# Decode signs, low parts and gate denominators on GpSimd in a windowed attention and rational FFN kernel

## The chip, the cores and the metric

The kernel runs on one core of one Trainium2 chip. The metric is the device time of one execution in microseconds; lower is better. Engines are named as in the profile: PE is TensorE (matrix products), DVE is VectorE, ACT is ScalarE, POOL is GpSimd, SP is SyncE, which issues all transfers here. Tiles lie in SBUF; matrix products land in PSUM.

## The reference, cut to what matters

Eight batches of eight heads attend over 576 positions of 64 dimensions, causally and within a window of 64. The attention output, 4608 tokens by 512, goes through a feed-forward layer of 2048 with a rational function as its gate.

```python
# attention
mask = (rel >= 0) & (rel < window)               # window = 64
scores = np.where(mask, scale * q @ k.T, -1e9)
attn = softmax(scores)
x = (attn @ v)                                   # 4608 x 512 after the heads are joined
# feed-forward
h = x @ w_in                                     # 512 x 2048
P = a[0] + a[1]*h + a[2]*h**2 + a[3]*h**3
Q = 1.0 + np.abs(b[0])*np.abs(h) + np.abs(b[1])*h**2
g = P / (Q + 1e-6)
return (g @ w_out).astype(np.float32)            # 2048 x 512
```

`w_in` and `w_out` are float64; everything else is float32.

## The kernel before, in words

Tokens are worked through in 12 chunks of 384 (`CH`), `c` = 0 to 11. A chunk has four attention units (`hp`, two heads each) and 16 feed-forward steps (`i`, 128 of the 2048 inner columns each). A unit computes scores into PSUM, adds the mask and takes row maxima (L185 to L206; in chunks 1 and 2, `PEM`, the mask is added by TensorE), exponentials with row sums on ScalarE (L210, L213), reciprocals and the scaling of the tile `sm` (L215 to L217), transposes on TensorE, and the product with v. Its result x is kept as two float32r parts, `xh` and `xl`.

A step (`ffn1`) multiplies x with a column block of `w_in` in three passes of high and low parts, 12 matrix products into the PSUM tile `h`. Then comes the gate: ScalarE makes |h|, a3 h + a2 and the start of the denominator, `u` (L258 to L260); VectorE makes the numerator from `h` in PSUM (L261, L262); `u` is multiplied by |h| (L264), on VectorE for the first 28 gates (`DEC`) and on GpSimd for the rest; ScalarE turns it into a reciprocal by logarithm and exponential (L267, L268); VectorE makes the gate's high and low parts `gh` and `gl` (L269 to L272). Three steps later (`LAG`) `ffn2` multiplies them with a row block of `w_out`, nine matrix products into three PSUM tiles `o` (L292). At a chunk's end ScalarE copies `o` out, or VectorE adds it to a part sum (L299 to L306). The phases run chunk 0's first half, chunk 1's first half, chunk 1's second half, chunk 0's second half, then chunks 2 to 11 whole.

Weights are float64 and are turned into two float32r parts on the chip, in 32 tiles (16 of each matrix), by `decode`: a transfer into `w_st` (two buffers), on ScalarE the magnitude of the high word scaled by a power of two (L117), on VectorE a left shift (L119), the low word's top bits (L120) and the sign bit (L121) into `w_c`, on ScalarE the high part (L124), on VectorE the rest (L125). Eight such tiles of each matrix are asked for in the first steps, the rest one per step from step 7 on; a list `todo` tells at which step each load and each attention unit is written. The order on each engine is then set by a scheduler that runs when the kernel is built; on the chip each engine works through its own queue in order.

Of the kernel before, what the change touches and what calls it, by code (L numbers as in the profile page):

```python
# [9 lines left out]
F32 = mybir.dt.float32  # L10
F32R = mybir.dt.float32r
U32 = mybir.dt.uint32
AF = mybir.ActivationFunctionType
ALU = mybir.AluOpType
# [3 lines left out]
CH = 384  # L18
TC = CH // WIN
PR = TC // 2  # L20
DEC = 28
AHEAD = 3
LAG = 3
W_AT = 0, 1, 2, 3
# [7 lines left out]
def swa_rational_ffn(ctx: ExitStack, tc: tile.TileContext, qT, kT, v, w_in, w_out, a, b, out):  # L32
    nc = tc.nc
    P = 128
# [9 lines left out]
    SCALE = 1.0 / math.sqrt(64)  # L44
# [50 lines left out]
    nc.scalar.copy(out=ident_r, in_=ident)  # L95


    wi_h = const.tile([P, NCC, DFF], F32R, name="wi_h")
    wi_l = const.tile([P, NCC, DFF], F32R, name="wi_l")
    wo_h = const.tile([P, NF, DO], F32R, name="wo_h")  # L100
    wo_l = const.tile([P, NF, DO], F32R, name="wo_l")
    w_out_v = w_out.rearrange("(fc p) e -> p fc e", p=P)

    def decode(src, hi, lo):

        w = stage.tile([P, 512, 2], U32, name="w_st", bufs=2)
        if len(src.shape) == 3:
            nc.sync.dma_start(out=w.rearrange("p (c n) two -> p c (n two)", c=src.shape[1]), in_=src)
        else:
            nc.sync.dma_start(out=w.rearrange("p n two -> p (n two)"), in_=src)  # L110
        low, high = w[:, :, 0], w[:, :, 1]
        c = stage.tile([P, 512], U32, name="w_c")
        cf = c.bitcast(F32)

        nc.scalar.activation(cf, w.bitcast(F32)[:, :, 1], AF.Abs, scale=2.0 ** -111)  # L117

        nc.vector.tensor_scalar(out=c, in0=c, scalar1=3, scalar2=None, op0=ALU.logical_shift_left)  # L119
        nc.vector.scalar_tensor_tensor(out=c, in0=low, scalar=29, in1=c, op0=ALU.logical_shift_right, op1=ALU.bitwise_or)  # L120
        nc.vector.scalar_tensor_tensor(out=c, in0=high, scalar=0x80000000, in1=c, op0=ALU.bitwise_and, op1=ALU.bitwise_or)  # L121
        if len(hi.shape) == 3:
            cf = cf.rearrange("p (c n) -> p c n", c=hi.shape[1])
        nc.scalar.activation(hi, cf, AF.Copy, scale=2.0 ** -8)  # L124
        nc.vector.scalar_tensor_tensor(out=lo, in0=cf, scalar=2.0 ** -8, in1=hi.bitcast(F32), op0=ALU.mult, op1=ALU.subtract)  # L125

# [2 lines left out]
        decode(w_in[i], wi_h[:, :, sl], wi_l[:, :, sl])  # L129

    def load_w_out(i):
        decode(w_out_v[:, i, :], wo_h[:, i, :], wo_l[:, i, :])

    xh, xl = {}, {}
    live = {}
# [37 lines left out]
    def unit_scores(c, hp):  # L173
        u = live[c, hp]

        ps = ps_a.tile([P, 2, 512], F32, name="ps_s", bufs=1)
        m0 = u["m0"]
        on_pe = c in PEM
        if m0 is None:
            mm = mask[:, 1:2, :].broadcast_to([P, PR, P])  # L180
        else:
            mm = mask[:, m0:m0 + PR, :]
        if on_pe:
            for z in range(2):
                nc.tensor.matmul(ps[:, z, 0:PR * P].rearrange("p (r c) -> p r c", c=P), ident_r, mm, start=True, stop=False)  # L185
        for p in range(PR):
            for z in range(2):
                for e in range(2):
                    j = 2 * p + e
                    k = u["kt"][z * 64:z * 64 + 64].rearrange("p t s -> p (t s)")  # L190
                    w = u["kw"][j] * WIN
                    nc.tensor.matmul(ps[e * 64:e * 64 + 64, z, p * P:(p + 1) * P], u["q"][z * 64:z * 64 + 64, j, :],  # L192
                                     k[:, w:w + P], start=not on_pe, stop=not on_pe or p == PR - 1)
        sm = att.tile([P, 2 * PR, P], F32, name="sm")
        NR = 2 * PR
        nmx = att.tile([P, NR], F32, name="nmx")
        if on_pe:
            pss = ps[:, :, 0:PR * P].rearrange("p z (r c) -> p z r c", c=P)
            nc.vector.tensor_reduce(out=nmx.rearrange("p (z r) -> p z r", z=2), in_=pss, axis=AX.X, op=ALU.max, negate=True)
            nc.vector.tensor_scalar(out=nmx, in0=nmx, scalar1=SCALE, scalar2=None, op0=ALU.mult)  # L200
        else:
            for z in range(2):
                nc.vector.scalar_tensor_tensor(out=sm[:, z * PR:(z + 1) * PR, :],
                                               in0=ps[:, z, 0:PR * P].rearrange("p (r c) -> p r c", c=P), scalar=SCALE,
                                               in1=mm.bitcast(F32), op0=ALU.mult, op1=ALU.add)
            nc.vector.tensor_reduce(out=nmx, in_=sm, axis=AX.X, op=ALU.max, negate=True)  # L206
        sums = att.tile([P, NR], F32, name="sums")
        for j in range(NR):
            if on_pe:
                nc.scalar.activation(sm[:, j, :], ps[:, j // PR, (j % PR) * P:(j % PR + 1) * P], AF.Exp, scale=SCALE,  # L210
                                     bias=nmx[:, j:j + 1], accum_out=sums[:, j:j + 1])
            else:
                nc.scalar.activation(sm[:, j, :], sm[:, j, :], AF.Exp, bias=nmx[:, j:j + 1], accum_out=sums[:, j:j + 1])  # L213
        rs = att.tile([P, NR], F32, name="rs")
        nc.vector.tensor_scalar(out=sums, in0=sums, scalar1=1e-9, scalar2=None, op0=ALU.add)  # L215
        nc.vector.reciprocal(out=rs, in_=sums)  # L216
        (nc.vector if c < 2 else nc.gpsimd).tensor_tensor(out=sm, in0=sm, in1=rs.unsqueeze(2).broadcast_to([P, NR, P]), op=ALU.mult)  # L217
        u["sm"] = sm

    def unit_transpose(c, hp):  # L220
# [20 lines left out]
        nc.vector.tensor_tensor(out=xl[c, hp], in0=x, in1=xh[c, hp].bitcast(F32), op=ALU.subtract)  # L241

    gs = {}
    n_gates = [0]

    def ffn1(c, i):
        h = ps_h.tile([P, CH], F32, name="h")
        n = 0
        for cc in range(NCC):
            for w, x in ((wi_h, xl), (wi_h, xh), (wi_l, xh)):  # L250
                nc.tensor.matmul(h, w[:, cc, i * P:(i + 1) * P], x[c, cc], start=n == 0, stop=n == 3 * NCC - 1)  # L251
                n += 1
        ah = tmp.tile([P, CH], F32, name="ah")
        u = tmp.tile([P, CH], F32, name="u")
        num = tmp.tile([P, CH], F32, name="num")
        gh = gp.tile([P, CH], F32R, name="gh")
        gl = gp.tile([P, CH], F32R, name="gl")
        nc.scalar.activation(ah, h, AF.Abs)  # L258
        nc.scalar.activation(num, h, AF.Identity, scale=a_sb[:, 3:4], bias=a_sb[:, 2:3])  # L259
        nc.scalar.activation(u, ah, AF.Identity, scale=b_sb[:, 1:2], bias=b_sb[:, 0:1])  # L260
        nc.vector.tensor_tensor(out=num, in0=num, in1=h, op=ALU.mult)  # L261
        nc.vector.scalar_tensor_tensor(out=num, in0=num, scalar=a_sb[:, 1:2], in1=h, op0=ALU.add, op1=ALU.mult)  # L262
        n_gates[0] += 1
        (nc.vector if n_gates[0] <= DEC else nc.gpsimd).tensor_tensor(out=u, in0=u, in1=ah, op=ALU.mult)  # L264


        nc.scalar.activation(ah, u, AF.Ln, bias=QADD)  # L267
        nc.scalar.activation(ah, ah, AF.Exp, scale=-1.0)  # L268
        nc.vector.scalar_tensor_tensor(out=gh, in0=num, scalar=a_sb[:, 0:1], in1=ah, op0=ALU.add, op1=ALU.mult)  # L269
        nc.vector.scalar_tensor_tensor(out=u, in0=u, scalar=QADD, in1=gh.bitcast(F32), op0=ALU.add, op1=ALU.mult)  # L270
        nc.vector.scalar_tensor_tensor(out=num, in0=num, scalar=a_sb[:, 0:1], in1=u, op0=ALU.add, op1=ALU.subtract)  # L271
        nc.vector.tensor_tensor(out=gl, in0=num, in1=ah, op=ALU.mult)  # L272
        gs[c, i] = gh, gl
# [8 lines left out]
    def ffn2(s):  # L282
        c, i = steps[s]
        first = s == 0 or steps[s - 1][0] != c
        last = s == total - 1 or steps[s + 1][0] != c
        if first:
            acc[c] = [ps_o.tile([P, DO], F32, name=f"o{t}") for t in range(NTS)]
        gh, gl = gs.pop((c, i))
        for t in range(NTS):
            ts = slice(t * P, (t + 1) * P)  # L290
            for n, (g, w) in enumerate(((gl, wo_h), (gh, wo_l), (gh, wo_h))):
                nc.tensor.matmul(acc[c][t], g[:, ts], w[:, i, :], start=first and n == 0, stop=last and n == 2)  # L292
        if not last:
            return
        o = acc.pop(c)
        if c == 0 and c not in part:
            part[c] = const.tile([P, NTS, DO], F32, name="part")
            for t in range(NTS):
                nc.scalar.copy(out=part[c][:, t, :], in_=o[t])  # L299
            return  # L300
        for t in range(NTS):
            ob = part[0][:, t, :] if s == total - 1 else op.tile([P, DO], F32, name="ob")
            if c in part:
                nc.vector.tensor_tensor(out=ob, in0=o[t], in1=part[c][:, t, :], op=ALU.add)
            else:
                nc.scalar.copy(out=ob, in_=o[t])  # L306
            nc.sync.dma_start(out=out[c * CH + t * P:c * CH + (t + 1) * P, :], in_=ob)

    NU = HP
# [93 lines left out]
```

## Time and profile before

| | us |
|---|---|
| median of 3 runs | 1017.18 (1016.14 to 1017.22) |
| profiled execution | 1016.97 |
| its span, first to last instruction | 1015.2 |
| TensorE busy | 950.6 |
| VectorE busy | 837.1 |
| ScalarE busy | 723.9 |
| GpSimd busy | 233.2 |
| mean granted TensorE clock | 0.984 |

In the profile's rows a group stands as line, engine, operation, tile written <- tiles read, shape, count, then busy us and mean ns of one, then the engine's idle time just before such instructions with what ended it. In the 40 slices each digit is a busy share in tenths. A row of the waits has the waiting engine and line, what it waited for, the total in us, the number of times and the longest. In a timeline row the first two numbers are start and duration in us.

### The profile page before, as it was taken

The numbers are of one execution on the slowest core, as the hardware profiler recorded it, in microseconds if no ns is written. First come the engines' busy times: TensorE is split into PE (matmuls) and PEld (weight loads), VectorE is DVE, ScalarE is ACT, GpSimd is POOL, SyncE is SP. The second block draws the span as 40 slices with busy tenths as digits, with TensorE's granted clock in tenths as the row PEclk, the third lists the DMA queues.
The fourth block names the chain that finished last, engine by engine and source line by source line (L and its number), as shares of the span: only waits on it lengthen the run. The fifth ranks groups of instructions, "written<-read, shape, count | busy, mean of one in ns | idle before, by whom it ended". The sixth has DMA issues, their size and how long they took to land.

```text
span 1015.2 us, 18235 instructions
## 1 busy us (share of the span) xinstructions
PE 950.6 (94%) x6640; PEld 839.4 (83%) x6640; DVE 837.1 (82%) x1599; ACT 723.9 (71%) x1736; POOL 233.2 (23%) x231
## 2 busy tenths in 40 slices
PE   2668768999999999999999999999999999999997
PEld 2556557988888988988988888988988888888996
DVE  5999899887988887788888888788788888877875
ACT  4677676666677777777777777777777777776664
POOL 2000000003223223223223223223223222222221
PEclk9979889999999999999999999999999999999998
DMA  6653540020121121120121111120121121100000
GB/s 192 201 168 130 171 151 17 1 76 31 60 61 30 61 64 33 65 60 30 61 61 31 62 63 34 64 61 29 60 60 32 62 62 34 65 17 1 32 1 31
DMA packets 37816, 64.08 MB, mean 63 GB/s; under 512 B 4448, under 2 KB 24928, under 8 KB 37728
## 3 DMA queue, kind: packets, MB, share of 16 engines
q1 hardware_dynamic: 37728, 62.93, 19.7%
q8 instruction: 52, 0.85, 0.4%
q14 instruction: 36, 0.29, 0.1%
HBM read 53.48 MB, written 9.44 MB: 62 GB/s over the span
## 4 chain that ended last, share of the span: by engine, by line
PE 78%; DVE 11%; ACT 5%; DMA 4%; issue 2%; POOL 0%; SPq 0%; POOLq 0%; ACTq 0%; DVEq 0%
PE o L292 35%; PE h L251 34%; PE ps_x L235 3%; PE ps_s L192 3%; PE ps_s L224 2%; DMA w_st<-w_in 2%; DVE gh L269 1%; DMA w_st<-w_out 1%; ACT sm L213 1%; DVE u L270 1%; DVE w_c L120 1%; DVE num L271 1%; DVE w_c L121 1%; ACT w_c L117 1%; DVE gl L272 1%
## 5 line engine op out<-in xcount | busy, mean ns | idle before, releaser
L251 PE MATMUL h<-xl,wi_h 128*128 128x384 f32 x768 | 265.7, 346 | 18.7 <-DVE num L262 15.3
L251 PE MATMUL h<-xh,wi_l 128*128 128x384 f32 x768 | 260.5, 339 | 0.0
L251 PE MATMUL h<-xh,wi_h 128*128 128x384 f32 x768 | 260.1, 339 | 0.0
L292 PE MATMUL o<-wo_h,gl 128*128 128x512 f32 x576 | 232.3, 403 | 15.0 <-DVE gl L272 15.0
L264 POOL TENSOR_TENSOR u<-u,ah 128x384 f32<-128x384 f32 x164 | 168.4, 1027 | 326.3 <-ACT u L260 286.2
L292 PE MATMUL o<-wo_h,gh 128*128 128x512 f32 x576 | 229.2, 398 | 0.0
L292 PE MATMUL o<-wo_l,gh 128*128 128x512 f32 x576 | 228.1, 396 | 0.0
L261 DVE TENSOR_TENSOR num<-num,h 128x384 f32<-128x384 f32 x192 | 106.1, 553 | 105.9 <-ACT num L259 105.1
L258 ACT ACTIVATE ah<-h 128x384 f32<-128x384 f32 x192 | 94.3, 491 | 115.0 <-PE h L251 86.8
L251 PEld LDWEIGHTS h<-xl,wi_h 128*128 128x128 f32 x768 | 145.8, 190 | 28.0 <-DVE num L262 18.1
L217 POOL TENSOR_TENSOR sm<-sm,rs 128x768 f32<-128x768 f32 x40 | 59.4, 1484 | 443.8 <-DVE rs L216 421.6
L251 PEld LDWEIGHTS h<-xh,wi_h 128*128 128x128 f32 x768 | 145.9, 190 | 4.2
L251 PEld LDWEIGHTS h<-xh,wi_l 128*128 128x128 f32 x768 | 145.6, 190 | 0.6 <-issue 0.2
L292 PEld LDWEIGHTS o<-wo_h,gl 128*128 128x128 f32 x576 | 109.3, 190 | 42.1 <-DVE gl L272 17.2
L213 ACT ACTIVATE sm<-sm,nmx 128x128 f32<-128x128 f32 x240 | 93.3, 390 | 62.7 <-DVE nmx L206 62.7
L269 DVE SCALAR_TENSOR_TENSOR gh<-num,a_sb,ah 128x384 fp32r<-128x384 f32 x192 | 117.2, 621 | 24.8 <-ACT ah L268 24.6
L260 ACT ACTIVATE u<-ah,b_sb 128x384 f32<-128x384 f32 x192 | 136.1, 710 | 0.0
L292 PEld LDWEIGHTS o<-wo_h,gh 128*128 128x128 f32 x576 | 109.5, 190 | 23.6
L259 ACT ACTIVATE num<-h,a_sb 128x384 f32<-128x384 f32 x192 | 128.3, 668 | 0.0
L292 PEld LDWEIGHTS o<-wo_l,gh 128*128 128x128 f32 x576 | 109.7, 190 | 18.9
L262 DVE SCALAR_TENSOR_TENSOR num<-num,a_sb,h 128x384 f32<-128x384 f32 x192 | 117.6, 613 | 5.4
L271 DVE SCALAR_TENSOR_TENSOR num<-num,a_sb,u 128x384 f32<-128x384 f32 x192 | 116.1, 618 | 0.5
(51 smaller groups left out, 1109.1 us busy)
## 6 DMA issues: line engine op xcount, KB each, us to landing
out<-ob SPq DMA_DIRECT2D x33, 256.0 KB, 2.4
w_st<-w_in SPq DMA_DIRECT2D x16, 512.0 KB, 4.2
w_st<-w_out SPq DMA_DIRECT2D x16, 512.0 KB, 3.7
q<-qT SPq DMA_DIRECT2D x32, 192.0 KB, 3.3
vt<-v SPq DMA_DIRECT2D x16, 384.0 KB, 3.1
vt<-v SPq DMA_DIRECT2D x16, 320.0 KB, 3.1
kt<-kT SPq DMA_DIRECT2D x16, 224.0 KB, 3.5
kt<-kT SPq DMA_DIRECT2D x16, 192.0 KB, 3.7
```

Of the source, the lines that this page charges most:

```text
L213: nc.scalar.activation(sm[:, j, :], sm[:, j, :], AF.Exp, bias=nmx[:, j:j + 1], accum_out=sums[:, j:j + 1])
L217: (nc.vector if c < 2 else nc.gpsimd).tensor_tensor(out=sm, in0=sm, in1=rs.unsqueeze(2).broadcast_to([P, NR, P]), op=ALU.mult)
L251: nc.tensor.matmul(h, w[:, cc, i * P:(i + 1) * P], x[c, cc], start=n == 0, stop=n == 3 * NCC - 1)
L258: nc.scalar.activation(ah, h, AF.Abs)
L259: nc.scalar.activation(num, h, AF.Identity, scale=a_sb[:, 3:4], bias=a_sb[:, 2:3])
L260: nc.scalar.activation(u, ah, AF.Identity, scale=b_sb[:, 1:2], bias=b_sb[:, 0:1])
L261: nc.vector.tensor_tensor(out=num, in0=num, in1=h, op=ALU.mult)
L262: nc.vector.scalar_tensor_tensor(out=num, in0=num, scalar=a_sb[:, 1:2], in1=h, op0=ALU.add, op1=ALU.mult)
L264: (nc.vector if n_gates[0] <= DEC else nc.gpsimd).tensor_tensor(out=u, in0=u, in1=ah, op=ALU.mult)
L269: nc.vector.scalar_tensor_tensor(out=gh, in0=num, scalar=a_sb[:, 0:1], in1=ah, op0=ALU.add, op1=ALU.mult)
L271: nc.vector.scalar_tensor_tensor(out=num, in0=num, scalar=a_sb[:, 0:1], in1=u, op0=ALU.add, op1=ALU.subtract)
L292: nc.tensor.matmul(acc[c][t], g[:, ts], w[:, i, :], start=first and n == 0, stop=last and n == 2)
```

## The change

Four things move. In `decode`, ScalarE copies the high word with its sign instead of taking its magnitude; GpSimd multiplies the high words by zero in place, which leaves the sign bit alone; the left shift and the setting of the sign become one VectorE instruction, so that two VectorE passes remain of three. For `w_out`, ScalarE's high part is a plain copy and GpSimd subtracts it to get the low part; both stay 256 times too large, and the factor is taken out where PSUM is emptied. The multiplication of L264 is done by GpSimd for all gates. The scaling of `sm` in chunk 1 goes to GpSimd as that of the later chunks does. Two small VectorE instructions with a constant take a tile of zeros as second operand.

```diff
+    zero = const.tile([P, 2 * PR], F32, name="zero")
+    nc.vector.memset(zero, 0.0)
...
-    def decode(src, hi, lo):
+    def decode(src, hi, lo, scaled=False):
...
-        nc.scalar.activation(cf, w.bitcast(F32)[:, :, 1], AF.Abs, scale=2.0 ** -111)
-
-        nc.vector.tensor_scalar(out=c, in0=c, scalar1=3, scalar2=None, op0=ALU.logical_shift_left)
+        highf = w.bitcast(F32)[:, :, 1]
+        nc.scalar.activation(cf, highf, AF.Copy, scale=2.0 ** -111)
+
+        nc.gpsimd.tensor_scalar(out=highf, in0=highf, scalar1=0.0, scalar2=None, op0=ALU.mult)
+        nc.vector.scalar_tensor_tensor(out=c, in0=c, scalar=3, in1=high, op0=ALU.logical_shift_left, op1=ALU.bitwise_or)
         nc.vector.scalar_tensor_tensor(out=c, in0=low, scalar=29, in1=c, op0=ALU.logical_shift_right, op1=ALU.bitwise_or)
-        nc.vector.scalar_tensor_tensor(out=c, in0=high, scalar=0x80000000, in1=c, op0=ALU.bitwise_and, op1=ALU.bitwise_or)
...
+        if scaled:
+            nc.scalar.copy(out=hi, in_=cf)
+            nc.gpsimd.tensor_tensor(out=lo, in0=cf, in1=hi.bitcast(F32), op=ALU.subtract)
+            return
...
-        decode(w_out_v[:, i, :], wo_h[:, i, :], wo_l[:, i, :])
+        decode(w_out_v[:, i, :], wo_h[:, i, :], wo_l[:, i, :], scaled=True)
...
-            nc.vector.tensor_scalar(out=nmx, in0=nmx, scalar1=SCALE, scalar2=None, op0=ALU.mult)
+            nc.vector.scalar_tensor_tensor(out=nmx, in0=nmx, scalar=SCALE, in1=zero, op0=ALU.mult, op1=ALU.add)
...
-        nc.vector.tensor_scalar(out=sums, in0=sums, scalar1=1e-9, scalar2=None, op0=ALU.add)
+        nc.vector.scalar_tensor_tensor(out=sums, in0=sums, scalar=1e-9, in1=zero, op0=ALU.add, op1=ALU.add)
...
-        (nc.vector if c < 2 else nc.gpsimd).tensor_tensor(out=sm, ...)
+        (nc.vector if c < 1 else nc.gpsimd).tensor_tensor(out=sm, ...)
...
-        n_gates[0] += 1
-        (nc.vector if n_gates[0] <= DEC else nc.gpsimd).tensor_tensor(out=u, in0=u, in1=ah, op=ALU.mult)
+        nc.gpsimd.tensor_tensor(out=u, in0=u, in1=ah, op=ALU.mult)
...
-                nc.scalar.copy(out=part[c][:, t, :], in_=o[t])
+                nc.scalar.activation(part[c][:, t, :], o[t], AF.Copy, scale=2.0 ** -8)
...
-                nc.vector.tensor_tensor(out=ob, in0=o[t], in1=part[c][:, t, :], op=ALU.add)
+                nc.vector.scalar_tensor_tensor(out=ob, in0=o[t], scalar=2.0 ** -8, in1=part[c][:, t, :], op0=ALU.mult, op1=ALU.add)
             else:
-                nc.scalar.copy(out=ob, in_=o[t])
+                nc.scalar.activation(ob, o[t], AF.Copy, scale=2.0 ** -8)
```

More of the change, by code (lines that the diff above doesn't have):

```diff
@@ L20 @@
 PR = TC // 2
-DEC = 28
 AHEAD = 3
@@ L214, in unit_scores @@
         rs = att.tile([P, NR], F32, name="rs")
-        nc.vector.tensor_scalar(out=sums, in0=sums, scalar1=1e-9, scalar2=None, op0=ALU.add)
+        nc.vector.scalar_tensor_tensor(out=sums, in0=sums, scalar=1e-9, in1=zero, op0=ALU.add, op1=ALU.add)
         nc.vector.reciprocal(out=rs, in_=sums)
-        (nc.vector if c < 2 else nc.gpsimd).tensor_tensor(out=sm, in0=sm, in1=rs.unsqueeze(2).broadcast_to([P, NR, P]), op=ALU.mult)
+        (nc.vector if c < 1 else nc.gpsimd).tensor_tensor(out=sm, in0=sm, in1=rs.unsqueeze(2).broadcast_to([P, NR, P]), op=ALU.mult)
         u["sm"] = sm
@@ L243, in swa_rational_ffn @@
     gs = {}
-    n_gates = [0]
     def ffn1(c, i):
```

## The prediction

> **What bounds the kernel now.** I read the page's totals and its 40 slices first, to see where TensorE isn't full, then busy times by stretch, then who waited for whom there, then the groups on VectorE, then single instructions of GpSimd beside those of VectorE.
>
> ```profile
> PE 950.6 (94%) x6640; PEld 839.4 (83%) x6640; DVE 837.1 (82%) x1599; ACT 723.9 (71%) x1736; POOL 233.2 (23%) x231
> PE   2668768999999999999999999999999999999997
> DVE  5999899887988887788888888788788888877875
> POOL 2000000003223223223223223223223222222221
> ```
>
> TensorE (PE) is full from the seventh slice on. Only the first six (25.4 us each) have holes, and there VectorE (DVE) is at 9 while GpSimd (POOL) has nothing after the mask. The same by stretch:
>
> ```profile
> core 0: us, PE busy (x) PEld busy (x) DVE busy (x) ACT busy (x) POOL busy (x), PEclk, DMA share, GB/s
> 10.00:52.00 42.00, 23.68 (x237) 18.75 (x238) 38.38 (x72) 26.90 (x80) 0.00 (x0) 1.00 0.62 189
> 52.00:163.00 111.00, 79.84 (x545) 66.20 (x545) 105.27 (x207) 78.59 (x195) 3.31 (x2) 0.88 0.43 139
> 163.00:240.00 77.00, 77.00 (x465) 68.10 (x464) 66.84 (x126) 51.10 (x115) 5.38 (x4) 1.00 0.10 31
> 240.00:950.00 710.00, 709.25 (x5088) 633.12 (x5087) 579.25 (x1112) 528.23 (x1276) 204.40 (x185) 1.00 0.16 49
> ```
>
> From 163 us on TensorE has no holes, so nothing that the change does there can shorten the run. All its effect comes from 10 to 163 us, where VectorE is busy 38.4 of 42 and 105.3 of 111 us. That VectorE is what TensorE waits for in the second of these, and ScalarE (ACT) too:
>
> ```profile
> PE h L251 <- DVE num L262: 15.3, 6, 6.3
> PE o L292 <- DVE gl L272: 12.0, 4, 4.6
> ACT wo_h L124 <- DVE w_c L121: 8.6, 6, 2.7
> ```
>
> TensorE's idle time there is 111 - 79.8 = 31.2 us, and 27.3 of it are these two VectorE releasers. So in this stretch a microsecond of VectorE is about a microsecond of the run, until ScalarE (78.6 us) or TensorE (79.8 us) is the next bound.
>
> The VectorE groups of 52 to 163 us that the change touches, or that matter below:
>
> ```profile
> L121 DVE SCALAR_TENSOR_TENSOR w_c<-w_st,w_c 128x512 uint32<-128x512 uint32 x21 | 14.2, 683 | 0.0
> L120 DVE SCALAR_TENSOR_TENSOR w_c<-w_st,w_c 128x512 uint32<-128x512 uint32 x21 | 14.1, 684 | 0.0
> L119 DVE TENSOR_SCALAR w_c<-w_c 128x512 uint32<-128x512 uint32 x21 | 8.8, 421 | 4.0 <-ACT w_c L117 4.0
> L125 DVE SCALAR_TENSOR_TENSOR wo_l<-w_c,wo_h 128x512 fp32r<-128x512 f32 x13 | 8.8, 678 | 0.1
> L262 DVE SCALAR_TENSOR_TENSOR num<-num,a_sb,h 128x384 f32<-128x384 f32 x14 | 8.3, 606 | 0.0
> L261 DVE TENSOR_TENSOR num<-num,h 128x384 f32<-128x384 f32 x14 | 7.5, 547 | 0.6 <-ACT num L259 0.5
> L264 DVE TENSOR_TENSOR u<-u,ah 128x384 f32<-128x384 f32 x13 | 7.1, 549 | 0.0
> L199 DVE TENSOR_REDUCE nmx<-ps_s 128x6 f32<-128x768 f32 x6 | 5.7, 950 | 0.0
> L217 DVE TENSOR_TENSOR sm<-sm,rs 128x768 f32<-128x768 f32 x4 | 3.8, 952 | 0.0
> L241 DVE TENSOR_TENSOR xl<-ps_x,xh 128x384 fp32r<-128x384 f32 x4 | 2.2, 550 | 0.0
> ```
>
> By itself this says that the change helps. What speaks against it is seen only in single instructions. Here are the two GpSimd instructions of that stretch, one of the later part, and the VectorE instructions beside them (start, duration):
>
> ```profile
> 132.92 0.65 DVE L125 SCALAR_TENSOR_TENSOR wo_l<-w_c,wo_h 128x512 fp32r<-128x512 f32 x1
> 133.19 1.72 POOL L217 TENSOR_TENSOR sm<-sm,rs 128x768 f32<-128x768 f32 x1 [124.82 <-DVE rs L216]
> 133.49 1.96 DVE L125 SCALAR_TENSOR_TENSOR wi_l<-w_c,wi_h 128x512 fp32r<-128x512 f32 x1
> ...
> 154.90 1.60 POOL L217 TENSOR_TENSOR sm<-sm,rs 128x768 f32<-128x768 f32 x1 [20.00 <-DVE rs L216]
> 155.08 1.83 DVE L270 SCALAR_TENSOR_TENSOR u<-u,gh 128x384 f32<-128x384 f32 x1
> ...
> 236.60 0.62 DVE L262 SCALAR_TENSOR_TENSOR num<-num,a_sb,h 128x384 f32<-128x384 f32 x1
> 237.06 1.02 POOL L264 TENSOR_TENSOR u<-u,ah 128x384 f32<-128x384 f32 x1 [2.65 <-ACT u L260]
> 237.43 1.06 DVE L269 SCALAR_TENSOR_TENSOR gh<-num,a_sb,ah 128x384 fp32r<-128x384 f32 x1 [0.21 <-ACT ah L268]
> ...
> 238.61 0.56 DVE L270 SCALAR_TENSOR_TENSOR u<-u,gh 128x384 f32<-128x384 f32 x1
> 239.74 0.61 DVE L269 SCALAR_TENSOR_TENSOR gh<-num,a_sb,ah 128x384 fp32r<-128x384 f32 x1
> ```
>
> GpSimd's multiply at 133.19 ends at 134.91. The VectorE subtraction begun at 133.49 takes 1.96 us instead of about 0.68 and ends at 135.45: it stood still until GpSimd was done. The second case is the same (1.83 instead of 0.56, ending 0.41 us after GpSimd's 156.50), and so is L269 at 237.43 (1.06 instead of 0.61, ending 0.41 us after 238.08). L262 at 236.60, which reads h from PSUM, is not lengthened by the GpSimd multiply that begins in it. So in these rows a VectorE instruction with both inputs in SBUF and a GpSimd instruction don't run together, and VectorE pays up to the whole GpSimd duration. The Trainium skill, "SBUF — State Buffer", section "Who interferes with whom", states it as a rule: a VectorE instruction with two SBUF inputs contends with a GpSimd instruction that reads SBUF, the later one standing until the first is done; the trace agrees, with 1.96 for 0.68 us. By the same page the faster modes of VectorE's one-input instructions contend too, which would make the removal of the 421 ns shift a gain of its own; no run here shows that.
>
> **The change, part by part.** What moves goes to an engine that is slower at it and that stops VectorE while it runs. Start-to-start, a VectorE instruction costs some 0.08 us less than its duration (133.49 against 132.92 + 0.65), which I take off each. Counts are those of 52 to 163 us.
>
> - Signs: three VectorE passes per tile become two. L119 goes, and the new first pass is a 684 ns one like L120. Relief 21 x (0.42 - 0.08) = 7.2 us.
> - w_out's low parts: 13 x (0.68 - 0.08) = 7.8 us.
> - Denominators (L264): 13 x (0.55 - 0.08) = 6.1 us.
> - The softmax scaling of chunk 1 (L217, the change has c < 1 for c < 2): 4 x (0.95 - 0.08) = 3.5 us.
>
> Relief 24.6 us, leaving VectorE 105.3 - 24.6 = 80.7 us. Added to GpSimd, by its own rows:
>
> ```profile
> L264 POOL TENSOR_TENSOR u<-u,ah 128x384 f32<-128x384 f32 x164 | 168.4, 1027 | 326.3 <-ACT u L260 286.2 <-PE ps_s L192 33.5 <-DVE num L261 5.8
> L217 POOL TENSOR_TENSOR sm<-sm,rs 128x768 f32<-128x768 f32 x40 | 59.4, 1484 | 443.8 <-DVE rs L216 421.6 <-ACT ah L258 22.2
> L78 POOL TENSOR_SCALAR_AFFINE_SELECT sm<-sm 64x128 f32<-64x128 f32 x10 | 2.9, 288 | 0.3
> L69 POOL MEMSET sm<- 128x640 f32 x1 | 0.6, 631 | 0.3 <-POOLq L393 0.3
> masks.py:197 POOL MEMSET ident<- 128x128 f32 x1 | 0.2, 204 | 0.1
> ```
>
> - 13 denominators x 1.02 = 13.3 us; 4 scalings x 1.47 = 5.9 us.
> - 13 low parts of 512 columns: at least a denominator's 1.03 us, at most 512/384 of it, 1.37. I take 1.27, as two full inputs are nearest to L264: 16.5 us.
> - 21 signs, one input, 512 columns at every other word. From below 0.5 us (the fill's 631 x 512/640), from above 1.37 (the two-input pace). The select has one input as well: 0.29 us at 128 columns, and the two fills give 0.83 ns for each further column, so 0.61 at 512. I take 0.65: 13.7 us. The Trainium skill, "GPSIMD Engine Reference", section 7, gives some 1.9 cycles per element for reads of this step; estimated from it the sign is 0.81 us, which would add 2.2 us to the result below; no run here shows it.
>
> Together 49.4 us of GpSimd. Call f the part of it for which VectorE stands. Relief and blocking cancel at f = 24.6 / 49.4 = 0.50. The rows give f from 0.44 (L269: 1.06 - 0.61 of 1.02, where the rest fell on L262) to 0.87 (1.96 - 0.68 of 1.47). VectorE can work unharmed only in what reads at most one operand from SBUF: L261, L262, L199 and L241, without the 0.08, make 6.5 + 7.4 + 5.2 + 1.9 = 21.0 us, to which its 5.7 idle us come; so even the best packing leaves f = (49.4 - 26.7) / 49.4 = 0.46. I take 0.65, the middle of 0.44 and 0.87, since the instructions around a decode are mostly of the blocked kind. The stretch becomes 80.7 + 0.65 x 49.4 + 5.7 = 118.5 us, 7.5 longer. At f = 0.46 it is 1.9 us shorter, at 0.87 18.4 longer.
>
> The stretch to 52 us, by the same durations:
>
> ```profile
> L119 DVE TENSOR_SCALAR w_c<-w_c 128x512 uint32<-128x512 uint32 x11 | 4.7, 424 | 12.2 <-ACT w_c L117 12.2
> L125 DVE SCALAR_TENSOR_TENSOR wo_l<-w_c,wo_h 128x512 fp32r<-128x512 f32 x4 | 2.7, 684 | 0.0
> ```
>
> Relief 11 x 0.34 + 4 x 0.60 = 6.2 us; GpSimd 11 x 0.65 + 4 x 1.27 = 12.2 us; at 0.65 this is 7.9 - 6.2 = 1.7 longer (-0.6 to +4.4).
>
> Edits at nothing: the denominators after 163 us lie under a full TensorE; without that cover each of the remaining 15 would cost what it does above. The small six-column instructions change form, not number. ScalarE's Abs becomes a Copy of the same size; the 2^-8 at PSUM's emptying rides on instructions that are there already, and so on full TensorE, three of the last chunk excepted. No transfer is added, but the sign is one more step ahead of the release of w_st, which the load two tiles on waits for, with the q, k and v loads queued behind that load on SyncE, and of all that is queued behind the first decode pass on VectorE; the queue rival below prices this.
>
> Sum: 7.5 + 1.7 = 9.2 us on the profiled execution's 1017.0 us (its span is 1015.2; the median, 1017.2, is 0.2 above): 1026.
>
> **The rivals.**
> - Hidden after all, faster. If the order puts GpSimd's work mostly beside PSUM reads and waits, or decodes slide behind 163 us, where VectorE has 77 - 66.8 = 10.2 us to spare, f falls to perhaps 0.25: 80.7 + 12.4 + 5.7 = 98.8, 12.2 us shorter, and 12.2 x 0.25 - 6.2 = -3.1 before: 1002. For it: L262 at 236.60 is untouched, and decodes are done well ahead of use. Against: both GpSimd instructions in the dense stretch blocked VectorE nearly in full. It decides below f = 0.46.
> - No measurable change, f near 0.5: 1015 to 1019.
> - The queue. GpSimd runs in order; a sign behind a low part that waits for ScalarE holds the next tile's VectorE pass and with it every gate behind that. At half a microsecond for each of 32 tiles this adds 16 us: 1042. For it: VectorE already waits 12.2 + 4.0 us for L117, the step that the sign follows; against: two tiles are in flight.
>
> **How the numbers follow.** The forecast (1019 to 1036) has 0.39, the queue 0.11, no change 0.13, hidden 0.37. About 0.2% (2 us) is what a measurement of this kernel can tell from no change. So slower 0.50, same 0.13, faster 0.37. The range leaves out a tenth on each side: most of the hidden case down to 998, and up to 1040, which is f = 0.87 in both stretches (1017.0 + 18.4 + 4.4).
>
> **What would show it.** Right: VectorE instructions with two SBUF inputs of over 1 us by the dozen before 170 us, ending some 0.4 us after a GpSimd instruction, while L261 and L262 keep theirs; TensorE's last hole later than 163 us; the rest of the run equally long. Wrong: such instructions are few, or the sign is far under 0.5 us, or VectorE's busy time in the head falls by 20 us and TensorE's holes go with it.

## The result, and the profile after

The changed kernel takes 1028.7 us (1028.45 to 1029.8) against 1017.2 us: a ratio of 1.0121, with a 95% interval of 1.0109 to 1.0133. It is 11.5 us slower; the forecast was 1026. The profiled execution takes 1028.45 us, its span 1026.7. The page of the changed kernel, its totals and three rows of its slices:

```profile
PE 953.7 (93%) x6640; PEld 841.9 (82%) x6640; DVE 832.7 (81%) x1520; ACT 725.3 (71%) x1736; POOL 348.5 (34%) x311
PE   2668667999999999999999999999999999999997
DVE  5889789878888878778778878878878878877875
POOL 5566466322323322322322322322322322322221
```

GpSimd is now busy 4 to 6 tenths of the head. In both pages the seventh slice is the last in which TensorE has a hole (8 tenths before, 7 now). Over the whole run VectorE is busy 4.4 us less than before (837.1), in a span 11.5 us longer: it stands idle 15.9 us more. Busy times by stretch, in the columns used before, and two rows from a finer division:

```profile
10.00:52.00 42.00, 22.53 (x242) 17.72 (x242) 35.58 (x56) 27.50 (x80) 19.97 (x12) 0.92 0.59 186
52.00:163.00 111.00, 78.66 (x528) 65.62 (x529) 96.36 (x143) 72.08 (x182) 69.14 (x47) 0.83 0.41 129
163.00:240.00 77.00, 70.02 (x413) 60.56 (x412) 63.79 (x109) 49.92 (x106) 29.69 (x24) 0.96 0.14 44
240.00:950.00 710.00, 710.00 (x5095) 634.17 (x5094) 580.38 (x1114) 528.58 (x1283) 204.97 (x185) 1.00 0.16 48
```

```profile
175.00:200.00 25.00, 21.99 (x95) 19.02 (x96) 21.33 (x36) 16.61 (x41) 11.70 (x9) 0.86 0.00 1
200.00:225.00 25.00, 25.00 (x148) 22.35 (x147) 20.67 (x38) 16.22 (x32) 6.34 (x6) 1.00 0.06 17
```

TensorE is full from 200 us instead of 163, and from 240 us on the two are alike: the loss is all in the head. Between 52 and 163 us ScalarE is less busy too (72.1 for 78.6): in the changed head no engine is full.

By these rows TensorE stands idle for 58.8 us between 10 and 240 us, where it was 49.5: 9.3 of the 11.5 us. Its matrix products also take longer in the head. Over the run it is busy 953.7 us for the same 6640 products, 950.6 before, and its granted clock between 52 and 163 us is 0.83, 0.88 before. Behind a wait of 6.92 us the products of `h` take 0.52 us until 142 us, and only then 0.34:

```profile
136.44 0.69 PE L260 MATMUL h<-xl,wi_h 128*128 128x384 f32 x1 [6.92 <-DVE num L271]
136.93 0.52 PE L260 MATMUL h<-xh,wi_h 128*128 128x384 f32 x1
...
142.55 0.34 PE L260 MATMUL h<-xh,wi_h 128*128 128x384 f32 x1
```

So a long hole in TensorE is followed by slow products, as it was before the change (0.52 us from 132 to 136 us, behind a wait of 6.30). What TensorE waited for between 52 and 200 us:

```profile
PE o L300 <- DVE gl L280: 16.8, 7, 4.3
PE h L260 <- DVE num L271: 16.1, 7, 6.9
PE ps_s L234 <- POOL sm L227: 6.7, 1, 6.7
```

The first two were 12.0 and 15.3 us. The third is a single wait of the transposes for chunk 1's scaling, which was 0.2 us before. These are the scores, the scaling and the transposes of that unit:

```profile
110.00 0.89 PE L202 MATMUL ps_s<-kt,q 64*64 64x128 f32 x24
119.94 1.47 POOL L227 TENSOR_TENSOR sm<-sm,rs 128x768 f32<-128x768 f32 x1 [2.90 <-ACT wi_h L134]
121.47 1.54 PE L234 MATMUL ps_s<-ident,sm 128*128 128x128 f32 x6 [6.74 <-POOL sm L227]
```

From the start of the scores to the end of the scaling 11.4 us pass. It is the eighth attention unit of the run. In the kernel before, the eighth unit's scores begin at 100.48 us and its scaling, on VectorE, ends at 116.18, after 15.7 us, yet its transposes at 118.31 wait for nothing: TensorE has 45 feed-forward products between the scores and the transposes there, and 15 here. So this hole goes with another order of TensorE's instructions, made when the kernel was built, and not with a longer softmax.

Groups of GpSimd and then of VectorE up to 200 us (in the changed kernel L124 is the sign, L132 the low part, L272 the denominator, L227 the scaling; L125 and L126 are the two decode passes, L135 the low part of w_in, L277 and L279 two passes of the gate, L270 and L271 the two that read h from PSUM):

```profile
L124 POOL TENSOR_SCALAR w_st<-w_st 128x512 f32<-128x512 f32 x32 | 54.9, 1720 | 37.1 <-ACT w_c L121 33.2 <-DVE w_c L126 2.2 <-DVE sm L213 1.7
L132 POOL TENSOR_TENSOR wo_l<-w_c,wo_h 128x512 fp32r<-128x512 f32 x16 | 24.8, 1550 | 16.0 <-ACT wo_h L131 16.0
```

```profile
L125 DVE SCALAR_TENSOR_TENSOR w_c<-w_c,w_st 128x512 uint32<-128x512 uint32 x32 | 27.5, 860 | 11.1 <-POOL w_st L124 10.9
L126 DVE SCALAR_TENSOR_TENSOR w_c<-w_st,w_c 128x512 uint32<-128x512 uint32 x32 | 24.1, 752 | 0.3
L135 DVE SCALAR_TENSOR_TENSOR wi_l<-w_c,wi_h 128x512 fp32r<-128x512 f32 x16 | 16.7, 1043 | 3.3 <-ACT wi_h L134 3.2
L277 DVE SCALAR_TENSOR_TENSOR gh<-num,a_sb,ah 128x384 fp32r<-128x384 f32 x18 | 15.8, 876 | 3.9 <-ACT ah L276 3.9
L279 DVE SCALAR_TENSOR_TENSOR num<-num,a_sb,u 128x384 f32<-128x384 f32 x18 | 15.4, 855 | 0.1
L271 DVE SCALAR_TENSOR_TENSOR num<-num,a_sb,h 128x384 f32<-128x384 f32 x19 | 11.5, 607 | 0.3
L270 DVE TENSOR_TENSOR num<-num,h 128x384 f32<-128x384 f32 x19 | 10.4, 547 | 4.3 <-ACT num L268 4.1
```

The VectorE groups with two inputs in SBUF have grown (L135 from its usual 0.68 to 1.04 us, L277 and L279 from 0.61 to 0.88 and 0.86), and the two that read PSUM have not (0.61 and 0.55). Single instructions show the same stop as before at a low part, and a shorter one at a sign:

```profile
96.20 1.65 POOL L132 TENSOR_TENSOR wo_l<-w_c,wo_h 128x512 fp32r<-128x512 f32 x1 [2.91 <-ACT wo_h L131]
96.64 1.62 DVE L279 SCALAR_TENSOR_TENSOR num<-num,a_sb,u 128x384 f32<-128x384 f32 x1
...
44.95 3.18 POOL L124 TENSOR_SCALAR w_st<-w_st 128x512 f32<-128x512 f32 x2 [2.69 <-ACT w_c L121]
46.58 1.17 DVE L125 SCALAR_TENSOR_TENSOR w_c<-w_c,w_st 128x512 uint32<-128x512 uint32 x1 [2.01 <-POOL w_st L124]
47.78 0.69 DVE L126 SCALAR_TENSOR_TENSOR w_c<-w_st,w_c 128x512 uint32<-128x512 uint32 x1
...
53.69 1.57 POOL L124 TENSOR_SCALAR w_st<-w_st 128x512 f32<-128x512 f32 x1 [0.18 <-ACT w_c L121]
54.16 0.75 DVE L135 SCALAR_TENSOR_TENSOR wi_l<-w_c,wi_h 128x512 fp32r<-128x512 f32 x1 [0.62 <-ACT wi_h L134]
```

L279 ends at 98.26, 0.41 us after the low part. The second of the two signs that begin at 44.95 ends at 48.13, but L125 at 46.58 loses only 0.49 us and L126 at 47.78 runs beside it unharmed; L135, begun 0.47 us into a sign, loses 0.07. So in these rows a sign of some 1.55 us stops VectorE in about its first half microsecond only; beside signs alone no instruction up to 225 us loses more than 0.49 us.

I added up, over the timeline to 225 us, by how much VectorE instructions beside a GpSimd one exceed their line's usual duration:

| GpSimd's part | count | its time, us | VectorE lengthened, us | for each | VectorE work spared by each |
|---|---|---|---|---|---|
| signs | 32 | 55.0 | 5.8 | 0.18 | 0.34 |
| low parts | 16 | 24.8 | 12.1 | 0.76 | 0.60 |
| denominators | 25 | 28.0 | 6.5 | 0.26 | 0.47 |
| scalings | 7 | 10.7 | 8.4 | 1.20 | 0.87 |

Together 32.8 us. A VectorE instruction that stands beside two GpSimd ones can be put down to either: shared out by how long each overlaps it, the signs come to 8.5 us and the scalings to 6.0, and the sum stays the same within 0.1. Three of the seven scalings are chunk 2's and ran on GpSimd before, too. The sum nearly cancels what was spared, which is why VectorE's busy time hardly moved. The rest is waiting. What VectorE waited for up to 225 us, the kernel before first, then the changed one (waiting line, releaser, us in total, times, longest):

```profile
DVE w_c L119 <- ACT w_c L117: 16.2, 12, 9.7
DVE num L261 <- ACT num L259: 5.9, 10, 1.1
DVE wi_l L125 <- ACT wi_h L124: 0.3, 1, 0.3
DVE gh L269 <- ACT ah L268: 0.2, 1, 0.2
```

```profile
DVE w_c L125 <- POOL w_st L124: 10.9, 9, 2.4
DVE sm L213 <- ACT mask L79: 7.9, 1, 7.9
DVE num L270 <- ACT num L268: 6.4, 9, 1.2
DVE gh L277 <- ACT ah L276: 4.9, 7, 1.5
DVE wi_l L135 <- ACT wi_h L134: 3.2, 6, 1.4
```

The longest wait in the first list (9.7) and the second row of the second list (7.9) are the wait at the very start. Behind it, VectorE waited 6.5 us for L117 before and now waits 10.9 us for the signs in its place, and it waits 4.9 and 3.2 us for ScalarE at gates and high parts, where it hardly waited before.

### The profile page after: what moved, and what is told of

The parts are those of the page before. It is cut to its first block, busy times and chain, and to the rows that moved or that the text cites. A ratio compares the mean times of both kernels' runs of the same rounds, so it can differ in the third digit from the quotient of the medians.

```text
span 1026.7 us, 18304 instructions
## 1 busy us (share of the span) xinstructions
PE 953.7 (93%) x6640; PEld 841.9 (82%) x6640; DVE 832.7 (81%) x1520; ACT 725.3 (71%) x1736; POOL 348.5 (34%) x311
## 4 chain that ended last, share of the span: by engine, by line
PE 81%; DVE 8%; ACT 4%; DMA 2%; issue 2%; POOL 2%; SPq 0%; POOLq 0%; ACTq 0%; DVEq 0%
PE o L300 36%; PE h L260 36%; PE ps_x L245 3%; PE ps_s L202 3%; PE ps_s L234 3%; DMA w_st<-w_in 2%; DVE w_c L125 1%; DVE gh L277 1%; POOL w_st L124 1%; ACT sm L220 1%; DVE u L278 1%; DVE w_c L126 1%; DVE num L279 1%; ACT w_c L121 1%; DVE wi_l L135 1%
## 5 line engine op out<-in xcount | busy, mean ns | idle before, releaser
L272 POOL TENSOR_TENSOR u<-u,ah 128x384 f32<-128x384 f32 x192 | 199.0, 1037 | 377.2 <-ACT u L269 327.5
L260 PE MATMUL h<-xl,wi_h 128*128 128x384 f32 x768 | 265.9, 346 | 20.9 <-DVE num L271 16.1
L260 PE MATMUL h<-xh,wi_l 128*128 128x384 f32 x768 | 261.0, 340 | 0.0
L260 PE MATMUL h<-xh,wi_h 128*128 128x384 f32 x768 | 260.9, 340 | 0.0
L270 DVE TENSOR_TENSOR num<-num,h 128x384 f32<-128x384 f32 x192 | 106.2, 553 | 110.0 <-ACT num L268 109.2
L260 PEld LDWEIGHTS h<-xl,wi_h 128*128 128x128 f32 x768 | 146.3, 191 | 29.7 <-DVE num L271 18.6
L260 PEld LDWEIGHTS h<-xh,wi_h 128*128 128x128 f32 x768 | 146.5, 191 | 4.6
L260 PEld LDWEIGHTS h<-xh,wi_l 128*128 128x128 f32 x768 | 146.3, 191 | 0.6 <-issue 0.2
L277 DVE SCALAR_TENSOR_TENSOR gh<-num,a_sb,ah 128x384 fp32r<-128x384 f32 x192 | 123.0, 650 | 27.7 <-ACT ah L276 27.7
L227 POOL TENSOR_TENSOR sm<-sm,rs 128x768 f32<-128x768 f32 x44 | 65.3, 1485 | 235.2 <-DVE rs L226 225.7
L271 DVE SCALAR_TENSOR_TENSOR num<-num,a_sb,h 128x384 f32<-128x384 f32 x192 | 117.8, 613 | 5.9
L279 DVE SCALAR_TENSOR_TENSOR num<-num,a_sb,u 128x384 f32<-128x384 f32 x192 | 120.1, 639 | 0.7
```

Of the source, the lines that this page charges most:

```text
L227: (nc.vector if c < 1 else nc.gpsimd).tensor_tensor(out=sm, in0=sm, in1=rs.unsqueeze(2).broadcast_to([P, NR, P]), op=ALU.mult)
L272: nc.gpsimd.tensor_tensor(out=u, in0=u, in1=ah, op=ALU.mult)
```

## The experiments

Two theories. A: GpSimd's reads stop VectorE, and that is the cost. B: the new step in each tile's chain and GpSimd's queue, which runs in order, are the cost, whatever it reads. Ratios are to the kernel before, run on the same chip, with 95% intervals; its median was 1016.6 to 1017.2 us from chip to chip. The instruction order of each kernel is made anew when it is built. On TensorE only one of the twelve kernels below, the control with the subtraction left on VectorE, keeps the order of the kernel before (over its first 1300 products); the other eleven leave it within the first 280. So each difference below but the control's holds an edit and a new order together, and no run measures the order by itself.

**Each part by itself, on the kernel before.** Only the signs (the new first lines of `decode` from the change, the low parts of both matrices as before):

> The kernel before with only the signs moved: ScalarE copies the high word, GpSimd multiplies it by zero, two VectorE passes remain. In the changed kernel a sign lengthened VectorE instructions by 5.8 us over 32 signs, while 32 x 0.34 = 10.9 us of VectorE work went. Theory A, only the time for which VectorE stands beside GpSimd counts: 5 us faster, about 1012. Rival B, the extra step in the chain of each tile and GpSimd's queue in order are the cost: 5 to 12 us slower, 1022 to 1029, with VectorE's idle time before the first pass grown.

1018.3 us, ratio 1.0017 (1.0001 to 1.0033). Neither: A was 6 us too low and B almost 4 too high. Its executions lie far apart, from 1013.7 to 1021.2.

Only the low parts (the lines that make them; the factor of 256 is taken out as in the change):

```diff
+        if scaled:
+            nc.scalar.copy(out=hi, in_=cf)
+            nc.gpsimd.tensor_tensor(out=lo, in0=cf, in1=hi.bitcast(F32), op=ALU.subtract)
+            return
```

> The kernel before with only w_out's low parts moved (scaled by 256 until PSUM is emptied). In the changed kernel each blocked VectorE for 0.76 us and spared it 0.60. Theory A: 16 x 0.16 = 2.6 us slower, about 1020. Rival B has no wait here, as no VectorE instruction follows a low part: within 2 us of 1017. A third view, that the freed 0.60 us counts and nothing else: 9.6 us faster, 1007.

1024.8 us, ratio 1.0081 (1.0066 to 1.0096). None of the three: the low parts alone cost 8 us, three times what A gave. GpSimd's group of low parts in this kernel:

```profile
L126 POOL TENSOR_TENSOR wo_l<-w_c,wo_h 128x512 fp32r<-128x512 f32 x16 | 25.8, 1618 | 117.8 <-ACT wo_h L125 117.8
```

In this kernel's trace no engine's wait is put down to a low part, so its place in GpSimd's queue isn't seen to hold anybody up. Up to 225 us TensorE waits less for VectorE's `num` and `gl` than in the kernel before (24.0 us for 27.3), but more for ScalarE's copies of the transposes (`pT`, 12.8 for 4.9).

Even VectorE's left shift, which reads one tensor, is stopped beside the low parts. From this kernel's timeline:

```profile
80.94 1.51 POOL L126 TENSOR_TENSOR wo_l<-w_c,wo_h 128x512 fp32r<-128x512 f32 x1 [1.71 <-ACT wo_h L125]
81.23 1.52 DVE L119 TENSOR_SCALAR w_c<-w_c 128x512 uint32<-128x512 uint32 x1
136.36 1.47 DVE L119 TENSOR_SCALAR w_c<-w_c 128x512 uint32<-128x512 uint32 x1
```

It takes 0.42 us otherwise. This bears out what the Trainium skill, "SBUF — State Buffer", section "Who interferes with whom", says of VectorE's faster modes, which no run had shown at the time of the prediction.

Only the denominators (`DEC = 0`):

> The kernel before with only the first 28 denominators moved. In the changed kernel each blocked VectorE for 0.34 us and spared it 0.47. Theory A: 13 x 0.13 = 1.7 us faster in the dense stretch, about 1015. Rival B: the hop from ScalarE to GpSimd and back delays gates that are three steps from use, no cost: 13 x 0.47 = 6 us faster, 1011.

1015.1 us, ratio 0.9986 (0.9974 to 0.9998). As A gave, though by no firm reading: in this kernel's own trace 27 denominators lengthen VectorE's instructions by 12.5 us, shared out by overlap, 0.46 each, where A took 0.34.

Denominators and the scaling of chunk 1 (`DEC = 0`, `c < 1`):

> The kernel before with the first denominators and the scaling of chunk 1 moved, signs and low parts not. Undoing these two in the changed kernel gave 7.6 us. If they cost that by themselves (VectorE standing beside them): 1020 to 1025. If only together with the signs and low parts, whose queue on GpSimd they share: 1015 to 1018, as the denominators alone gave 1015.

1017.8 us, ratio 1.0010 (1.0000 to 1.0021): little by themselves.

**A control for the low parts.** w_out scaled by 256, the subtraction left on VectorE:

```diff
-            nc.gpsimd.tensor_tensor(out=lo, in0=cf, in1=hi.bitcast(F32), op=ALU.subtract)
+            nc.vector.tensor_tensor(out=lo, in0=cf, in1=hi.bitcast(F32), op=ALU.subtract)
```

> The kernel before with w_out scaled by 256 until PSUM is emptied, as in the run with the low parts moved, but the low parts stay on VectorE as a plain subtraction. If the 8 us of that run come from GpSimd making the low parts: 1016 to 1018. If they come from the scaling or from another order of the instructions: 1022 to 1026.

1016.65 us, ratio 0.9997 (0.9988 to 1.0007). The scaling and the new exit from PSUM cost nothing. What costs is that GpSimd subtracts, or the other order that comes with it: this kernel keeps TensorE's old order, the one with GpSimd's subtractions doesn't.

**Fills in place of reads.** Low parts filled instead of subtracted, so that w_out's low parts are left out of the result:

```diff
-            nc.gpsimd.tensor_tensor(out=lo, in0=cf, in1=hi.bitcast(F32), op=ALU.subtract)
+            for _ in range(3):
+                nc.gpsimd.memset(lo.bitcast(F32), 0.0)
```

> The run with only the low parts moved (1024.8 us), with each GpSimd subtraction replaced by three GpSimd fills of the low part with zero, which read nothing; w_out's low parts are left out of the result that way. GpSimd's place, its waits and about its time stay. If the reading is what costs: the 8.7 us by which VectorE instructions were lengthened go, and the 9.6 us spared on VectorE show, 1008 to 1014. If another order of the instructions or the wait for ScalarE's high part costs: 1022 to 1026.

1014.0 us, ratio 0.9973 (0.9961 to 0.9986). GpSimd's fills in this kernel, their group first and then a row of the timeline:

```profile
L127 POOL MEMSET wo_l<- 128x512 f32 x48 | 23.8, 543 | 0.1
12.81 19.86 POOL L127 MEMSET wo_l<- 128x512 f32 x40
```

Three fills take as long as one subtraction (3 x 0.54 against 1.62 us), but they are not in its place. A fill reads nothing, so it needn't wait for ScalarE's high part, and all 48 run between 6 and 33 us, ahead of the dense stretch, while the subtractions ran from 27 to 157 us. So the waits that the expectation meant to keep are gone with the reads, and this run can't tell a read from a step in the queue. It shows what the run takes when the low parts are taken off both engines: 10.8 us less than with GpSimd's subtractions, and 3 us less than the kernel before, where VectorE makes them. TensorE's waits for VectorE's `num` and `gl` up to 225 us are 13.7 us here, against 24.0 with the subtractions. As no engine is seen to wait for a subtraction, what is left as its cost is VectorE's standing, 8.7 us by the count of the table, and the other order. Beside the early fills the one-input shift, 0.42 us alone, takes up to 0.74:

```profile
16.13 0.74 DVE L119 TENSOR_SCALAR w_c<-w_c 128x512 uint32<-128x512 uint32 x1 [1.02 <-ACT w_c L117]
```

Signs as fills in the changed kernel, three and one for each, so that the signs are left out of the weights:

```diff
-        nc.gpsimd.tensor_scalar(out=highf, in0=highf, scalar1=0.0, scalar2=None, op0=ALU.mult)
+        nc.gpsimd.memset(highf, 0.0)    # three times, or once
```

> The changed kernel with each sign (one GpSimd instruction of 1.55 us that reads and writes the high words) replaced by three GpSimd fills of the same words with zero, which read nothing; all weights come out positive. The step, its place in the queue and about its length stay, the reading goes. Theory A (VectorE stands while GpSimd reads): the 5.8 us of lengthened VectorE instructions at the signs go, 1023. Rival B (the step and GpSimd's queue are the cost): 1027 to 1030, VectorE's waits for the sign unchanged near 11 us.

1018.6 us, ratio 1.0021 (1.0011 to 1.0031).

> As before, but one fill in place of each sign, so a third of the time: all weights come out positive. Theory A: as with three fills, 1023. Rival B: GpSimd's head load falls by about 32 us and the step by 1 us per tile, and with them VectorE's 13 us of added idle time before the 24th gate: 1012 to 1018.

1016.5 us, ratio 0.9998 (0.9984 to 1.0013). Of the kernel with three fills, one of the three groups of fills, and VectorE's wait for them:

```profile
L124 POOL MEMSET w_st<- 128x512 f32 x32 | 18.0, 565 | 35.8 <-ACT w_c L121 35.4 <-POOL w_st L124 0.3
```

```profile
DVE w_c L127 <- POOL w_st L126: 9.5, 7, 2.4
```

These fills do stand where the signs stood: they wait for L121 (35.4 us) as the signs did (33.2). No VectorE instruction that stands beside them alone is lengthened, by the count of the table. The step is as long (3 x 0.566 us against 1.72), VectorE still waits 9.5 us for it, and 10.1 us are gone. So VectorE's waiting for signs is not the price. What went is the reading, for which A has 5.8 us, and with the new order TensorE's wait of 6.7 us for the scaling: the eighth unit's transposes wait for nothing here. The run doesn't part the two. A fill a third as long brings 2.1 us more.

**Parts undone in the changed kernel.** Signs made by ScalarE; this kernel, too, leaves the signs out of the weights:

```diff
-        nc.gpsimd.tensor_scalar(out=highf, in0=highf, scalar1=0.0, scalar2=None, op0=ALU.mult)
+        nc.scalar.activation(highf, highf, AF.Copy, scale=0.0)
```

> The changed kernel with the signs made by ScalarE (the high words times zero in place), 32 x 0.67 = 21 us more on ScalarE, nothing read by GpSimd and no step on another engine. Theory A: 5.8 us less than the changed kernel, 1023. Rival B: also free of the wait for GpSimd, 1012 to 1018. Third: ScalarE, 72 of 111 us busy in the stretch from 52 us, becomes late itself: over 1028.

1021.0 us, ratio 1.0040 (1.0026 to 1.0054), between A's and B's values, with 32 x 0.67 us more on ScalarE. Its order has a hole of its own: transposes that stand right behind their scores wait 4.7 us for the exponentials.

Denominators and scaling back on VectorE (`n_gates <= 28`, `c < 2`):

> The changed kernel with the first 28 denominators and the scaling of chunk 1 back on VectorE, signs and low parts still on GpSimd. Theory A: denominators cost 13 x 0.13 = 1.7 us more and the scalings 4 x 0.33 = 1.3 us less: unchanged, 1028 to 1030. Rival B: GpSimd's queue loses 17 instructions and 19 us ahead of the signs, so the signs come sooner: 1020 to 1025.

1021.1 us, ratio 1.0044 (1.0027 to 1.0061): 7.6 us less, where A gave none and B 4 to 9. TensorE's wait in front of the eighth unit's transposes is down to 1.0 us here.

Low parts back on VectorE (the edit of the control, in the changed kernel):

> The changed kernel with w_out's low parts back on VectorE, still scaled by 256; signs, denominators and scaling stay on GpSimd. If the parts add up, the 8 us that the low parts cost alone come back: 1020 to 1022. If the low parts matter only as one of the four that share GpSimd's queue, more comes back: 1014 to 1019. If VectorE's regained work weighs more there than the reads do: 1026 or over.

1015.1 us, ratio 0.9988 (0.9977 to 0.9998): 13.6 us less, more than the whole loss. The change without its low parts is about as fast as the kernel before, or a little faster. Its transposes wait for the scaling once, for 0.4 us.

Each by itself, the parts cost 8.0 (low parts), 1.6 (signs) and 0.8 us (denominators and scaling), 10.4 together, not far from the 11.5 of the whole. But undoing any one of them gives back 7.6 to 13.6 us, 29 for the three, and low parts with signs (denominators and scaling undone) cost 4.4 us, less than low parts alone. No price per part fits all of these. TensorE's wait of 6.7 us for the eighth unit may be part of the answer: none of the five kernels with a part undone has it, whichever part that was, though one has a like hole of 4.7 us elsewhere. What it is worth in the run's time no run shows.

**No denominator product at all.** It follows from A that VectorE's relief is worth most where nothing takes its place at the port. ScalarE's L260 can make a square, which makes the product unnecessary (not shown below: `st` is filled once, and its constant takes the place of QADD in L270, too):

```diff
-        nc.scalar.activation(u, ah, AF.Identity, scale=b_sb[:, 1:2], bias=b_sb[:, 0:1])
+        nc.scalar.activation(u, ah, AF.Square, scale=st[:, 0:1], bias=st[:, 1:2])
-        (nc.vector if n_gates[0] <= DEC else nc.gpsimd).tensor_tensor(out=u, in0=u, in1=ah, op=ALU.mult)
-        nc.scalar.activation(ah, u, AF.Ln, bias=QADD)
+        nc.scalar.activation(ah, u, AF.Ln, bias=st[:, 2:3])
```

> The kernel before without any product u |h|: ScalarE's instruction that makes the start of the denominator makes (s|h| + t) squared instead, with s the root of |b1| and t = |b0| / 2s, and 1 - t squared goes into the constant. VectorE is spared the 28 instructions of L264 (13 x 0.47 = 6 us in the dense stretch) and GpSimd all 164 of its own, so nothing takes their place at the shared port. If VectorE's time is the bound of the head: 5 to 7 us faster, 1010 to 1012. If the waits between engines are: within 2 us of 1017.

1015.2 us, ratio 0.9985 (0.9976 to 0.9994). Faster, but by 1.8 us instead of 5 to 7. Its stretch of 52 to 163 us, and what TensorE waited for there:

```profile
52.00:163.00 111.00, 80.72 (x536) 68.21 (x536) 100.32 (x192) 78.55 (x195) 3.59 (x2) 0.82 0.43 135
PE o L299 <- DVE gl L279: 11.3, 5, 4.3
PE h L260 <- DVE num L271: 10.8, 2, 6.8
PE ps_s L233 <- ACT wo_h L133: 5.0, 1, 5.0
```

VectorE lost 5 us of work there (105.3 before), and TensorE's two waits for VectorE fell from 27.3 to 22.1 us, by as much. But one wait of 5.0 us came in front of transposes, again of the eighth unit, where the new order leaves 24 products between scores and transposes instead of 45. And TensorE, busy 80.7 us for 79.8 before, worked through 536 products for 545, at a granted clock of 0.82 for 0.88. So the relief did reach TensorE, and other things took it back; this run doesn't decide what a microsecond of VectorE in the head is worth.

## Why the prediction was right, and where it was not

- **The place: right.** The loss lies ahead of TensorE's full stretch. The prediction's reading of the slices was off by one (the seventh stands at 8 tenths, so seven have holes, not six); it went by the stretches, which are right.
- **The mechanism: seen as foretold, but not shown to be the whole cost.** VectorE instructions with two SBUF inputs stand until GpSimd has done, 29 of over 1 us before 170 us where there were 2, and those with PSUM inputs keep their times. The fills for signs show that VectorE's waiting for GpSimd is not the price there. But 6.7 us of TensorE's idle time, of which 9.3 were added, are one new wait that goes with another order of its instructions. The prediction didn't think of the order, and no run parts it from the standing.
- **The relief: right.** Counts and durations as forecast; the second decode pass of 684 ns is 0.68 us where nothing stops it.
- **The sign: the worst term.** Taken at 0.65 us and bounded by 1.37, it takes 1.53 to 2.00 us. It was also assumed to block like the others, 0.65 of its time; it blocks 0.18 us of it on the average, 5.8 us in all where the prediction put 32 x 0.65 x 0.65 = 13.5. The estimate from the Trainium skill, "GPSIMD Engine Reference", section 7, 0.81 us, was nearer, but half of it: the trace has 1.55. The 2.2 us that the prediction gives for it count the 21 signs of the dense stretch only; all 32 would add 3.3.
- **The share f: too high.** Low parts 12.1 / 24.8 = 0.49, scalings 0.79, denominators 0.23, against 0.65 for all; with the signs it is 32.8 / 118.5 = 0.28. With the longer signs the blocked time came out at 32.8 us where 32.1 + 7.9 = 40.0 was forecast.
- **Edits at nothing: the waits were not nothing.** By the forecast's own sum VectorE's busy time should have grown by 9 us; it fell by 4.4, and its idle time grew by 15.9.
- **The number: luck.** With the measured 32.8 us in the place of 40.0, the forecast's own sum (blocking less a relief of 24.6 + 6.2 = 30.8) gives 2 us, nearly no change. A blocking 7 us too large stood in for waits, an order and a slower TensorE priced at nothing. The queue rival named one of these waits (10.9 us for the signs, 4.4 more than VectorE had waited there before), but not as it works: three fills keep that wait and lose 10.1 us all the same.

What stays open: how much of the 11.5 us is VectorE's standing and how much the order, and why the parts give back so much more when undone than they cost when added. VectorE's added waits are for ScalarE and for signs, engines that wait for VectorE in turn, so a stop may be paid again when the answer comes back late; a long hole of TensorE is paid again in slower products (0.52 for 0.34 us). No run isolates either. A kernel with the change's instructions in the order of the kernel before would. Nor is it known what holds six of the twelve kernels between 1014 and 1017 us, where the kernel before is too, though VectorE's load in them differs by several microseconds.

## What to carry to other kernels

Before work goes from VectorE to GpSimd, compare what VectorE is spared with what GpSimd's instruction takes, since VectorE's instructions with two SBUF inputs stop for it: the kernel that moved 16 low parts, 0.60 us spared for 1.62 us moved each, was 8 us slower. Move what runs beside PSUM reads, or what only writes: fills as long as the signs lengthened no VectorE instruction that stood beside them alone. And before a difference is put down to an edit, compare the order of the instructions on the engine that bounds the run, and the waits that end last there: one hole of 6.7 us came and went with the order here, whichever part was edited.

## What the runs showed that was not expected

- A GpSimd product of 512 one-input columns at every other word, in place, takes 1.55 us, longer than a two-input one of 512 packed columns at its fastest (1.25), but stopped VectorE for no more than 0.49 us.
- GpSimd fills the same 512 columns, at every other word, in 0.57 us, packed ones in 0.54. Neither lengthened an instruction with two inputs that stood beside them alone; beside the packed ones the one-input shift took up to 0.74 us for 0.42.
- VectorE's one-input shift of 0.42 us is stopped by GpSimd's subtraction as well (1.52 and 1.47 us).
- Behind a wait of 6.92 us TensorE's products of 384 columns took 0.52 us until 5.6 us later, then 0.34.
